# The last stage of a long convolution in two column tiles, with tokens on other partitions

## The chip, the cores and the metric

The kernel runs on one core of a Trainium2 chip. The metric is the device time of one execution in microseconds (us); the time before is the median of three runs. A profile of one execution goes with it.

## The reference

Two pairs of layers work on 2048 tokens of 512 channels in bf16. The first layer of a pair, A, is a gated long convolution; the second, B, is a layer norm, a matrix product to 1376, a gelu, and a product back to 512. Each layer norms its input first and adds its result to it. Both pairs have the same weights, and k and v do not depend on x, so the convolution's result y is the same in both pairs:

```python
def _A_ref(q, k, v, shift_k, ssm_k, ssm_D):
    ...
    kv = k_shift * v          # k after a causal filter of 4 taps per channel
    kv_f = rfft2(kv_pad); kf_f = rfft2(kf_pad)
    y = irfft2(kv_f * kf_f)[:, :S]      # causal convolution over all 2048 tokens
    y = y + kv * ssm_D
    return q * y

x = A_q
x = x + A(layernorm(x), A_k, A_v, ...)
x = x + B(layernorm(x), ...)
x = x + A(layernorm(x), A_k, A_v, ...)
x = x + B(layernorm(x), ...)
```

## The kernel before, in words

**Layout.** The tokens are taken in two halves of 1024 (h = 0 and 1). In a half, partition p holds the eight tokens 8p to 8p + 7 (`HALF`, L165): `xh[h]` is [128, 8, 512] and holds q, then x, up to the end. Because a partition's eight tokens are neighbours in DRAM, a load of q (`lx0`, `lx1`, L483) reads 128 runs of 8 KB that follow each other, and a store of the result (`st...`, L648) writes 128 rows of 1 KB, 8 KB apart. There are two such loads, and sixteen stores of 128 KB.

**The convolution.** The spectrum of a half is built in stages of small transforms, each a matrix product with a table (F, W, M, G; `_make_tables`). After the first stage (tables F) the data is regrouped: for the first half by transposes on TensorE (L345, L353), for the second by a write to a DRAM buffer (`first_stage_dram`, L357; `zd`, L375) and a regrouped read that brings it back in another order (L411 for the filter, L475 for kv). Then come the second stage (W, L428 and L497), the product with the filter's spectrum on VectorE (L511), the inverse second stage (M, L523), and a second regrouping, again by sixteen transposes on TensorE for the first half (L538) and by a write and a regrouped read in DRAM for the second (L530, L532).

**The last stage (L543 to L549).** For each half and each of four groups of 128 channels (cc) a block of sixteen matmuls with the table G fills one PSUM tile of [128, 8, 128] f32: for each of eight token places n, two matmuls (gh = 0 and 1) with 128 x 128 weights accumulate into the same 128 partitions. The weights of gh are zero in all columns but those of its own tokens: column 4a + 2gh + gl is the token group of output partition p. So a block is `Y{h}{cc}`, and there are eight. The tile is evacuated by one instruction on ScalarE or VectorE (L263, L265) into `ya(h, cc)`, where the gate of layer A (L591, L592) multiplies it by the normed x.

**The layers.** A half has two groups of 512 tokens. Norm statistics run on VectorE (L284), the power on GpSimd (L297), the norm is applied on ScalarE or VectorE (L304, L306), the normed tokens go through a DRAM buffer (L608) and a transposing transfer (L611), and then come the two matrix products (L623, L640), the gelu (L630) and the residual (L644).

**Order.** Nothing is scheduled at run time: `ORDER` (L16) lists all pieces by hand with their engine (P, D, A, G, S) and their PSUM or SBUF slots, and every engine works through its own pieces in that order. Nearly all transfers are on the queue of S (SyncE, SP in the profile). In that order `lx0.S` stands just ahead of `K1w0.S`, the last write of the filter's first stage, and `K1r0.S`, its regrouped read, follows the weights of layer B; `lx1.S` stands behind `U1w2.S` and ahead of `U1w1.S`, writes of kv's first stage. `lx1` goes where kv was, so it waits for all first-stage matmuls of that half. `KW101.P`, the first matmuls behind `K1r0`, stands in TensorE's order ahead of the last two of these.

Of the kernel before, what the change touches and what calls it, by code (L numbers as in the profile page):

```python
# [9 lines left out]
BF16 = mybir.dt.bfloat16  # L10
# [53 lines left out]
NK = 16  # L64
# [8 lines left out]
def _make_tables():  # L73
    a = np.arange(NA)
    k1 = np.arange(NA)
    psi = 2 * np.pi * np.outer(a, k1 + 0.25) / NA
    C, S = np.cos(psi), np.sin(psi)


    F = np.zeros((128, 2, 256))  # L80
    for g in range(4):
        r = 4 * a + g
        F[r, 0, g * 64:g * 64 + 32] = C
        F[r, 0, g * 64 + 32:g * 64 + 64] = S
        F[r, 1, g * 64:g * 64 + 32] = S
        F[r, 1, g * 64 + 32:g * 64 + 64] = -C


    W = np.zeros((128, NK, 128))

    M = np.zeros((128, NK, 2, 128))
    b = np.arange(NA)
    k2 = np.arange(NA)
    g, n = b // 8, b % 8
    for ka in range(NK):
        for par in range(2):
            phi = 2 * np.pi * ((16 * par + ka + 0.25) * b / 1024)[:, None] + 2 * np.pi * np.outer(b, k2) / NA
            c, s = np.cos(phi), np.sin(phi)
            rr = n * 16 + g * 4 + par
            ri = rr + 2  # L100
            m0 = par * 32
            W[rr, ka, m0:m0 + 32] = c
            W[rr, ka, 64 + m0:64 + m0 + 32] = s
            W[ri, ka, m0:m0 + 32] = -s
            W[ri, ka, 64 + m0:64 + m0 + 32] = c
            vr = (par * 4 + (g % 2) * 2) * 16 + (g // 2) * 8 + n
            vi = vr + 16
            for q, sign in ((0, 1.0), (64, -1.0)):
                rows = np.arange(q + m0, q + m0 + 32)
                M[np.ix_(rows, [ka], [0], vr)] = (sign * c.T / 32)[:, None, None, :]  # L110
                M[np.ix_(rows, [ka], [0], vi)] = (-sign * s.T / 32)[:, None, None, :]
                M[np.ix_(rows, [ka], [1], vr)] = (s.T / 32)[:, None, None, :]
                M[np.ix_(rows, [ka], [1], vi)] = (c.T / 32)[:, None, None, :]


    G = np.zeros((128, 2, 128))
    for gh in range(2):
        for gl in range(2):
            for par in range(2):
                r = np.arange(NK) * 8 + par * 4 + gl * 2  # L120
                k = 16 * par + np.arange(NK)
                cols = 4 * a + 2 * gh + gl
                G[np.ix_(r, [gh], cols)] = C[:, k].T[:, None, :] / 32
                G[np.ix_(r + 1, [gh], cols)] = S[:, k].T[:, None, :] / 32
    return tuple(_to_bf16_uint16(t) for t in (F, W, M, G))


# [26 lines left out]
def kernel(ctx: ExitStack, tc: tile.TileContext, A_q, A_k, A_v, A_shift_k, A_ssm_k, A_ssm_D,  # L154
                 B_x, B_w1, B_b1, B_w2, B_b2, out):
    nc = tc.nc
    P = 128
    _, S, D = A_q.shape
    F = B_w1.shape[1]
    KS = A_shift_k.shape[1]  # L160
    NT = 8
# [1 line left out]
    FT = (F + P - 1) // P  # L163
    FL = F - (FT - 1) * P
    HALF = "(h p n) d -> h p n d"  # L165
    q_d, k_d, v_d, out_d = (t.flatten_outer_dims().rearrange(HALF, h=2, p=P) for t in (A_q, A_k, A_v, out))
    K = 1024
    NPS, NZT, NXB, NTB = 4, 6, 3, 3

    def apf(t, offset, dims):  # L170
        tensor = t.tensor if isinstance(t, bass.AP) else t
        return bass.AP(tensor=tensor, offset=offset, ap=[[int(s), int(c)] for s, c in dims])

    F_np, W_np, M_np, G_np = _make_tables()
    F_h = nc.inline_tensor(F_np, name="tabF")
# [55 lines left out]
    sT = const.tile([P, CT, KS], BF16, name="sT")  # L231
    sF = const.tile([P, CT, KS], F32, name="sF")
    Ft = const.tile([P, 2, 2 * P], BF16, name="Ft")
    Gt = const.tile([P, 2, P], BF16, name="Gt")
    Wt = const.tile([P, NK, P], BF16, name="Wt")
    B1 = const.tile([P, FT], F32, name="B1")
    b1T = const.tile([P, FT], BF16, name="b1T")
# [29 lines left out]
    def queue(eng):  # L267
        return {"S": nc.sync, "A": nc.scalar, "G": nc.gpsimd}[eng]
# [50 lines left out]
    add = plan.add  # L319
    with tc.tile_pool(name="ps", bufs=1, space=bass.MemoryType.PSUM) as ps:  # L320
        pf = [ps.tile([P, 1024], F32, name=f"p{i}") for i in range(NPS)]

        def load(name, dst, src, nbytes, deps=(), **info):
            return add(name, "S", deps, lambda it: queue(it["eng"]).dma_start(dst, src), nbytes=nbytes, **info)
# [10 lines left out]
        def zt(it):  # L335
            return ZTb[it["slot"]["zt"]]
# [49 lines left out]
        lk = [load(f"lk{h}", kn[h], k_d[h], 2 ** 20) for h in range(2)]  # L386
        lv = [load(f"lv{h}", uv[h], v_d[h], 2 ** 20) for h in range(2)]
        lW = load("lW", Wt[:], W_h.ap().bitcast(BF16), 2 ** 19)
        lG = load("lG", Gt[:], G_h.ap().bitcast(BF16), 2 ** 16)

        KTe, KT = [[], []], [[], []]
        KSp, KUp = [[], []], [[], []]
# [87 lines left out]
                                         ring="zt"))  # L480
        names = {it["name"]: it for it in plan.items}
        USall = [[names[f"U{h}S{n}"] for n in range(NT)] if UD[h] else [names[f"U{h}{cc}S{q}"] for cc in range(CT) for q in range(2)] for h in range(2)]
        lx = [load(f"lx{h}", xh[h], q_d[h], 2 ** 20, (KSall[0] + KSall[1]) if h == 0 else USall[1]) for h in range(2)]  # L483


        YE = [[], []]
# [2 lines left out]
        for h in range(2):  # L489
            for cc in range(CT):  # L490
# [52 lines left out]
                def mms(o, te=te):  # L543
                    for n in range(NT):
                        for gh in range(2):
                            nc.tensor.matmul(o[:, n, :], Gt[:, gh, :], view(zt(te), [16, P])[:, gh * 8 + n, :], start=gh == 0, stop=gh == 1)
                _, ev = mm_evac(f"Y{h}{cc}", mms, [NT, P], lambda it, h=h, cc=cc: ya(h, cc), [te, lG], USall[0] if h == 0 else (),
                                free_mm=[(te, "zt")], units=16)
                YE[h].append(ev)  # L549
# [25 lines left out]
        for i, (l, g) in enumerate(seq):  # L575
# [59 lines left out]
            for t in range(4):  # L635
# [9 lines left out]
                res[(l, g, t)] = add(f"re{i}{t}", "D", [pe], resid, free=[(pe, "ps")], ns=690)  # L645
                mm2p[i].append(pe)
                if l == 1:
                    add(f"st{i}{t}", "S", [res[(l, g, t)]], lambda it, h=h, n=n0 + t: queue(it["eng"]).dma_start(out_d[h][:, n, :], xh[h][:, n, :]),  # L648
                        nbytes=2 ** 17)
        with tc.manual_schedule(engines={ENG.PE, ENG.Activation, ENG.DVE, ENG.Pool, ENG.SP}):  # L650
            plan.write(ORDER)
# [30 lines left out]
```

## Time and profile before

| | |
|---|---|
| median of three runs | 278.54 us (278.10 to 279.81) |
| the profiled execution's own time | 278.57 us |
| its span, first to last instruction | 276.8 us |
| TensorE matmuls busy | 254.5 us |
| VectorE busy | 185.0 us |
| ScalarE busy | 156.5 us |
| moved by DMA | 39.53 MB |
| matmuls of the last stage (L546) | 128, 8.5 us busy |

How to read the profile: PE is TensorE's matmuls, PEld its weight loads, DVE VectorE, ACT ScalarE, POOL GpSimd, SP SyncE; a q behind a name is the engine's sequencer, which waits or issues a transfer. The row of 40 digits cuts the span into 40 slices of 6.92 us; a digit is the busy share in tenths, for DMA the mean over 16 DMA engines. The chain of waits is followed back from the last instruction, at each step to what released it. A load's line in the kernel is that of the helper (L324). `arena` is the one large SBUF tile, `p` the PSUM tiles.

### The profile page before, as it was taken

The numbers are of one execution on the slowest core, as the hardware profiler recorded it, in microseconds if no ns is written. First come the engines' busy times: TensorE is split into PE (matmuls) and PEld (weight loads), VectorE is DVE, ScalarE is ACT, GpSimd is POOL, SyncE is SP. The second block draws the span as 40 slices with busy tenths as digits, with TensorE's granted clock in tenths as the row PEclk, the third lists the DMA queues.
The fourth block names the chain that finished last, engine by engine and source line by source line (L and its number), as shares of the span: only waits on it lengthen the run. The fifth ranks groups of instructions, "written<-read, shape, count | busy, mean of one in ns | idle before, by whom it ended". The sixth has DMA issues, their size and how long they took to land.

```text
span 276.8 us, 5232 instructions
## 1 busy us (share of the span) xinstructions
PE 254.5 (92%) x2112; PEld 159.7 (58%) x2112; DVE 185.0 (67%) x357; ACT 156.5 (57%) x197; POOL 50.7 (18%) x95
## 2 busy tenths in 40 slices
PE   2699999999765988999999898999999999999994
PEld 2599999679733644785766443444444444444441
DVE  0499688977995799999896879920039998001021
ACT  0366328998885997368982495276502741754300
POOL 3860000000502046321400124110002332000000
PEclk9999999999997999999999999999999999999999
DMA  6994093237999999987199803753000114601011
GB/s 165 400 417 188 2 227 78 93 138 244 346 217 278 324 211 193 176 195 132 40 233 230 109 2 115 211 147 60 2 0 0 40 66 116 159 3 38 11 49 54
DMA packets 48843, 39.53 MB, mean 143 GB/s; under 512 B 32850, under 2 KB 44212, under 8 KB 47412
## 3 DMA queue, kind: packets, MB, share of 16 engines
q1 hardware_dynamic: 48066, 39.07, 55.0%
q8 instruction: 16, 0.26, 0.4%
q10 hardware_dynamic: 674, 0.14, 0.3%
q0 software_dynamic: 80, 0.00, 0.1%
q14 instruction: 7, 0.06, 0.1%
HBM read 19.28 MB, written 12.06 MB: 113 GB/s over the span
## 4 chain that ended last, share of the span: by engine, by line
PE 68%; DMA 19%; DVE 6%; SPq 2%; ACT 2%; issue 1%; ACTq 0%
PE p L623 24%; PE p L640 22%; DMA arena<-zd 6%; PE p L463 5%; PE p L523 3%; DMA arena<-in_A_q_dram 3%; PE p L345 3%; DVE lst L284 3%; PE p L353 3%; PE p L365 2%; DMA zd<-arena 2%; DMA arena<-in_A_ssm_k_dram 2%; DMA arena<-vd 2%; DMA arena<-lnd 2%; PE p L428 2%; SPq L608 2%
## 5 line engine op out<-in xcount | busy, mean ns | idle before, releaser
L263 ACT ACTIVATE arena<-p 128x1024 bf16<-128x1024 f32 (+1 forms) x75 | 77.0, 1085 | 39.7 <-PE p L345 10.4
L640 PE MATMUL p<-arena 128*128 128x512 bf16 (+1 forms) x352 | 78.0, 379 | 2.3 <-ACT arena L630 2.3
L623 PE MATMUL p<-arena 128*128 128x512 bf16 (+1 forms) x352 | 77.8, 379 | 1.2 <-ACT arena L630 0.8
L630 ACT ACTIVATE arena<-p,B 128x512 bf16<-128x512 f32 (+1 forms) x88 | 54.6, 687 | 25.8 <-PE p L623 25.8
L297 POOL TENSOR_TENSOR lrs<-lrs,mhalf 128x2 f32<-128x2 f32 x32 | 28.6, 894 | 172.0 <-DVE lnm L294 172.0
L644 DVE TENSOR_TENSOR arena<-p,arena 128x512 bf16<-128x512 f32 x32 | 21.8, 688 | 56.8 <-PE p L640 56.7
L640 PEld LDWEIGHTS <-arena 128*128 128x128 bf16 (+1 forms) x352 | 34.1, 98 | 42.9 <-issue 2.9
L623 PEld LDWEIGHTS <-arena 128*128 128x128 bf16 (+1 forms) x352 | 35.0, 100 | 41.0 <-issue 1.0
L284 DVE BATCH_NORM_STATS2 lst<-arena 128x6 f32<-128x512 bf16 x64 | 41.0, 683 | 3.1 <-DMA arena<-in_A_q_dram 2.6
L304 ACT ACTIVATE arena<-arena,lnm,lrs 128x512 bf16<-128x512 bf16 x32 | 24.1, 813 | 30.2 <-POOL lnm L298 30.2
L511 DVE TENSOR_TENSOR arena<-arena 128x2048 bf16<-128x2048 bf16 x24 | 28.7, 1220 | 2.3 <-PE p L523 1.9
L265 DVE COPY arena<-p 128x2048 bf16<-128x2048 bf16 (+1 forms) x16 | 18.8, 1186 | 13.8 <-PE p L398 10.4
L523 PE MATMUL p<-arena 128*128 128x128 bf16 x384 | 24.1, 219 | 0.1
L265 DVE CAST arena<-p 128x1024 bf16<-128x1024 f32 x19 | 23.0, 1219 | 1.5 <-PE p L523 0.5
L523 PEld LDWEIGHTS <-arena 128*128 128x128 bf16 x384 | 22.4, 98 | 2.3 <-DVE arena L511 0.5
L463 PE MATMUL p<-arena 128*128 128x128 bf16 x256 | 15.4, 219 | 0.0
L463 PEld LDWEIGHTS <-arena 128*128 128x128 bf16 x256 | 14.8, 98 | 0.1
L428 PE MATMUL p<-arena,Wt 128*128 128x256 bf16 x64 | 9.5, 283 | 4.4 <-DMA arena<-zd 3.6
L306 DVE TENSOR_SCALAR arena<-arena,lrs,lnm 128x512 bf16<-128x512 bf16 x32 | 11.6, 408 | 2.8 <-POOL lnm L298 2.8
L365 PE MATMUL p<-arena,Ft 128*128 128x512 bf16 x48 | 12.7, 400 | 0.6 <-ACT arena L263 0.6
L591 DVE TENSOR_TENSOR arena<-arena 128x1024 bf16<-128x1024 bf16 x16 | 11.0, 688 | 2.8 <-ACT arena L263 1.7
L398 PE MATMUL p<-IDt,arena 128*128 128x128 bf16 x64 | 6.2, 269 | 7.0 <-DMA arena<-in_A_ssm_k_dram 7.0
(42 smaller groups left out, 168.8 us busy)
## 6 DMA issues: line engine op xcount, KB each, us to landing
arena<-arena SPq DMA_DIRECT2D x8, 512.0 KB, 8.5
zd<-arena SPq DMA_DIRECT2D x8, 512.0 KB, 5.0
lnd<-arena SPq DMA_DIRECT2D x14, 256.0 KB, 2.3
arena<-in_A_ssm_k_dram SPq DMA_DIRECT2D x8, 256.0 KB, 7.4
arena<-in_A_k_dram SPq DMA_DIRECT2D x2, 1024.0 KB, 8.3
arena<-in_A_v_dram SPq DMA_DIRECT2D x2, 1024.0 KB, 13.5
arena<-in_A_q_dram SPq DMA_DIRECT2D x2, 1024.0 KB, 6.6
arena<-zd SPq DMA_DIRECT2D x2, 1024.0 KB, 18.1
```

Source lines behind the costliest of these rows:

```text
L263: nc.scalar.activation(dst, src, AF.Copy)
L265: nc.vector.tensor_copy(dst, src)
L284: nc.vector.bn_stats(self.st[:, i, :], xg[:, i, :])
L297: nc.gpsimd.tensor_tensor(self.rs[:, a:b], self.rs[:, a:b], mhalf[:, a:b], ALU.pow)
L304: nc.scalar.activation(dst[:, i, :], xg[:, i, :], AF.Identity, bias=bi, scale=sc)
L463: nc.tensor.matmul(o[:, n, :], kT[:, cc, (n - t) % NT, c:c + P], DG[:, cc, t, :], start=t == 0, stop=t == KS - 1)
L511: nc.vector.tensor_tensor(Tb[it["slot"]["T"]], x2, kk, ALU.mult)
L523: nc.tensor.matmul(o[:, i, :], *ab, start=s == 0, stop=s == n - 1)
L623: nc.tensor.matmul(o[0:m, x, :], W1t[:, ct, ft * P:ft * P + m], lt[:, ct, :], start=ct == 0, stop=ct == CT - 1)
L630: nc.scalar.activation(ht[0:m, ft, :], o[0:m, x, :], AF.Gelu_apprx_tanh, bias=B1[0:m, ft:ft + 1])
L640: nc.tensor.matmul(o, ht[0:m, ft, t * P:t * P + P], W2t[0:m, ft, :], start=ft == 0, stop=ft == FT - 1)
L644: nc.vector.tensor_tensor(xg[:, t, :], view(pf[pe["slot"]["ps"]], [D]), xg[:, t, :], ALU.add)
```

## The change

The two halves of the output columns (gh) become two column tiles of TensorE's array. One table G of 64 columns serves both: column 32gl + a. The matmul of gh writes PSUM partitions 64gh to 64gh + 63, each matmul starts and ends its own accumulation, and none adds to another's result. There are still sixteen matmuls in a block, each with its weight load, of 64 columns in place of 128.

So token group 4a + 2gh + gl now lies on partition 64gh + 32gl + a. For the gate, q has to lie in the same way, and the result goes back from there. `token_rows` describes it on the DRAM side: four groups, 8 tokens apart, of 32 rows, 32 tokens apart. k and v stay as they were, as do all earlier stages. Layer B and the norms work token by token, whatever the order of tokens on the partitions is.

The order of all instructions on all engines is unchanged; other than the matmuls of L546 and their weight loads, the load of G, the two loads of q and the sixteen stores, the instructions are the same.

```diff
-    G = np.zeros((128, 2, 128))
-    for gh in range(2):
-        for gl in range(2):
-            for par in range(2):
-                r = np.arange(NK) * 8 + par * 4 + gl * 2
-                k = 16 * par + np.arange(NK)
-                cols = 4 * a + 2 * gh + gl
-                G[np.ix_(r, [gh], cols)] = C[:, k].T[:, None, :] / 32
-                G[np.ix_(r + 1, [gh], cols)] = S[:, k].T[:, None, :] / 32
+    G = np.zeros((128, 64))
+    for gl in range(2):
+        for par in range(2):
+            r = np.arange(NK) * 8 + par * 4 + gl * 2
+            k = 16 * par + np.arange(NK)
+            cols = 32 * gl + a
+            G[np.ix_(r, cols)] = C[:, k].T / 32
+            G[np.ix_(r + 1, cols)] = S[:, k].T / 32
...
-    q_d, k_d, v_d, out_d = (t.flatten_outer_dims().rearrange(HALF, h=2, p=P) for t in (A_q, A_k, A_v, out))
+    k_d, v_d = (t.flatten_outer_dims().rearrange(HALF, h=2, p=P) for t in (A_k, A_v))
...
+    def token_rows(t, h, n0, n9):
+        return apf(t, (h * 1024 + n0) * D, [[8 * D, 4], [32 * D, 32], [1, (n9 - n0) * D]])
...
-    Gt = const.tile([P, 2, P], BF16, name="Gt")
+    Gt = const.tile([P, P // 2], BF16, name="Gt")
...
-        lG = load("lG", Gt[:], G_h.ap().bitcast(BF16), 2 ** 16)
+        lG = load("lG", Gt[:], G_h.ap().bitcast(BF16), 2 ** 15)
...
-        lx = [load(f"lx{h}", xh[h], q_d[h], 2 ** 20, (KSall[0] + KSall[1]) if h == 0 else USall[1]) for h in range(2)]
+        lx = [load(f"lx{h}", xh[h], token_rows(A_q, h, 0, NT), 2 ** 20, (KSall[0] + KSall[1]) if h == 0 else USall[1]) for h in range(2)]
...
-                            nc.tensor.matmul(o[:, n, :], Gt[:, gh, :], view(zt(te), [16, P])[:, gh * 8 + n, :], start=gh == 0, stop=gh == 1)
+                            nc.tensor.matmul(o[64 * gh:64 * gh + 64, n, :], Gt[:, :], view(zt(te), [16, P])[:, gh * 8 + n, :], start=True, stop=True)
...
-                    add(f"st{i}{t}", "S", [res[(l, g, t)]], lambda it, h=h, n=n0 + t: queue(it["eng"]).dma_start(out_d[h][:, n, :], xh[h][:, n, :]),
+                    add(f"st{i}{t}", "S", [res[(l, g, t)]], lambda it, h=h, n=n0 + t: queue(it["eng"]).dma_start(token_rows(out, h, n, n + 1), xh[h][:, n, :]),
```

## The prediction

> **What bounds the kernel now.** I read the page first (busy shares, the 40 slices, the shares of the chain), then the chain of waits in order of time, then the windows by stage.
>
> ```profile
> span 276.8 us, 5232 instructions
> PE 254.5 (92%) x2112; PEld 159.7 (58%) x2112; DVE 185.0 (67%) x357; ACT 156.5 (57%) x197; POOL 50.7 (18%) x95
> ...
> DMA  6994093237999999987199803753000114601011
> ...
> PE 68%; DMA 19%; DVE 6%; SPq 2%; ACT 2%; issue 1%; ACTq 0%
> ```
>
> TensorE is busy for 92% of the span and gives 68% of the chain; DMA gives 19%. The DMA row is nearly solid nines from its eleventh slice to its seventeenth (69 to 118 us): in the middle the bound is the transfers, not TensorE. The chain of waits, in order of time (start, us, what), says which ones:
>
> ```profile
> 62.20 6.71 DMA zd<-arena
> 68.98 16.11 DMA arena<-zd
> 85.13 1.03 PE p L428 x4
> ...
> 87.90 8.49 DMA arena<-in_A_q_dram
> ...
> 96.41 1.29 DVE lst L284 x2
> ...
> 126.57 6.24 PE p L623 x28
> ...
> 134.60 0.89 PE p L546 x16
> ...
> 149.06 0.52 PE p L546 x10
> 149.58 6.12 DMA arena<-vd
> ...
> 155.74 1.07 PE p L546 x16
> ...
> 158.54 0.89 PE p L546 x16
> ...
> 273.02 0.69 DVE arena L644
> ```
>
> A write of the first stage to DRAM (L375), its regrouped read (L411), four matmuls that waited for it, then the second load of q (8.49 us), then VectorE's statistics on that load: all of this one behind the other, up to 126.57, when TensorE becomes the chain. From there it is matmuls but for one wait for a regrouped read (149.58). The four L546 rows are the last stage's blocks of the second half (h=1), the only ones of its eight on the chain; a residual at 273.02 and a store end it.
>
> The load of q is not only waited for. All these transfers are issued by SP:
>
> ```profile
> 61.08 0.33 SPq L324 DMA_DIRECT2D arena<-in_A_q_dram  x1
> 62.20 0.32 SPq L375 DMA_DIRECT2D zd<-arena  x1
> ...
> 66.60 1.74 SPq L324 DMA_DIRECT2D arena<-in_B_w_dram  x2
> 68.98 10.87 SPq L411 DMA_DIRECT2D arena<-zd  x2
> ...
> 87.90 0.33 SPq L324 DMA_DIRECT2D arena<-in_A_q_dram  x1
> 88.33 2.84 SPq L375 DMA_DIRECT2D zd<-arena  x2
> ...
> 99.11 7.06 SPq L475 DMA_DIRECT2D arena<-zd  x3
> ...
> 124.49 0.58 SPq L532 DMA_DIRECT2D arena<-vd  x1
> ```
>
> The first load of q (61.08) goes out just ahead of the chain's write (62.20); the weights (66.60) follow and then the regrouped read (68.98), which waits for that write. The second (87.90) goes out just ahead of two writes (88.33) that the reads at 99.11 wait for. So q's bytes stand in front of chain bytes twice.
>
> ```profile
> core 0: us, PE busy (x) PEld busy (x) DVE busy (x) ACT busy (x) POOL busy (x), PEclk, DMA share, GB/s
> 13.50:20.50 7.00, 7.00 (x110) 6.84 (x109) 6.63 (x8) 4.84 (x4) 4.91 (x10) 1.00 1.02 416
> 62.20:69.00 6.80, 6.80 (x124) 6.80 (x122) 5.19 (x7) 6.05 (x6) 0.00 (x0) 1.00 0.77 243
> 87.90:96.40 8.50, 7.44 (x57) 5.02 (x57) 5.18 (x7) 8.50 (x11) 0.00 (x0) 0.97 1.02 343
> 96.40:112.50 16.10, 14.00 (x91) 7.30 (x89) 15.84 (x43) 13.99 (x21) 7.52 (x12) 1.00 1.17 195
> ...
> 273.70:276.80 3.10, 0.00 (x0) 0.00 (x0) 0.01 (x1) 0.00 (x0) 0.00 (x0) 0.89 0.12 42
> ```
>
> The last two columns are the mean busy share of 16 DMA engines, and GB/s. Where the inputs stream (13.50) one engine moves 416 / (1.02 x 16) = 25.5 GB/s; in the window of the second load 343 / (1.02 x 16) = 21.0. In the window of the first load the engines are idle for a share of 0.23, that is 1.6 of 6.80 us; from 87.90 to 112.50 they have no idle time. VectorE is busy for 15.84 of 16.10 us behind the second load: a delay at 96.41 is passed on.
>
> **The change, part by part.** First the transfers. token_rows turns the DRAM side of the two loads (L483) and the sixteen stores (L648) from 128 rows one after another into 4 groups of 32 rows with a stride; the on-chip side stays 128 partitions, and each row keeps its length (8 KB for a load, 1 KB for a store). In the changed kernel's instruction list the stores read 4x32x512 where they read 128x512. Bytes and number of pieces are the same; what can change is how a transfer is divided among the 16 engines. No transfer of before has a leading dimension of 4, so I bound it. One end: divided as before, 64 KB of a load on each engine, 65,536 / 25.5 = 2.6 us: no cost. Other end: the leading dimension is what is divided, so at most four engines get a share, 256 KB each: 262,144 / 25.5 = 10.3 us, or 12.5 at 21.0 GB/s. I take four shares. The nearest rows are the window's 1.02 of share at 416 GB/s, of transfers that all lead with 128 on both sides, and the regrouped reads of L411 and L475, whose DRAM side is written with a dimension of 16 in front: every wide transfer of this code leads with a multiple of 16 on both sides, and these are the first that don't.
>
> [...]
>
> Each load then keeps its engines for 10.3 - 2.6 = 7.7 us longer (12.5 - 3.1 = 9.4 at the lower rate).
>
> ```profile
> DMA to landing us min/median/max: 6.6/6.6/6.6
> ...
> DMA to landing us min/median/max: 1.9/1.9/3.2
> ```
>
> The first row is the first load of q (6.6 us), the second the stores (1.9 at best). A store has 8 KB on each engine, 0.3 us of its 1.9, so some 1.6 us are fixed.
>
> - First load. The write at 62.20 and the read at 68.98 have their parts on the same four engines behind it. At most the delay is 9.4; at least it is the bare load, 1.6 + 10.3 = 11.9, less 6.6 = 5.3. I take 7.7 less the 1.6 us of idle time in that window: 6.1 us on the chain, at 85.13.
> - Second load. At most 9.4; at least 11.9 - 8.49 = 3.4, if nothing stands before it. VectorE waits for it, and TensorE waits for the writes behind it (88.33, then 99.11). I take 4.6, nearer to the low end, since 8.49 is far above the bare 1.6 + 2.6 and part of it is a queue that a delay of the stage drains.
> - VectorE's statistics on the first load start as late as that load; what is queued behind them there (evacuations of the transposes of the first half, then L546) has until 85.13, when TensorE waited 3.55 us for the regrouped read.
>
> ```profile
> 75.67 2.18 PE L546 MATMUL p<-arena,Gt 128*128 128x128 bf16 x32 [1.49 <-DVE arena L265]
> ...
> 85.13 1.03 PE L428 MATMUL p<-arena,Wt 128*128 128x256 bf16 x4 [3.55 <-DMA arena<-zd]
> ```
>
> It costs nothing while that read is late by as much, and up to 7.7 less that 3.55, 4.2 us, if it is not.
> - Stores. Only the last one ends the span. It has 32 KB on each of four engines in place of 8: 24,576 bytes at 42 / (0.12 x 16) = 21.9 GB/s, 1.1 us. The others lie beside matmuls, where the DMA row shows sixes and less; without that cover each costs the same 1.1.
> - Issue. A transfer in a new form may take SP longer to issue: 0.33 us each now; the nearest with a split side is 0.58 (L532, one issue). 0.25 at the last store, taken as nothing.
>
> The table G shrinks from 64 to 16 KB; it is wanted at 68 us and was loaded in the first ten. Nothing.
>
> Second, the last stage, L546. Sixteen matmuls a block stay sixteen, with weights of 64 columns, to PSUM partitions 0 to 63 and 64 to 127 in turn, each complete by itself instead of accumulated in pairs.
>
> ```profile
> L353 PEld LDWEIGHTS <-arena 128*128 128x128 bf16 x128 | 9.0, 148 | 0.2
> ...
> L546 PEld LDWEIGHTS <-Gt 128*128 128x128 bf16 x128 | 7.6, 98 | 4.0 <-issue 2.0 <-DMA arena<-vd 1.5
> ...
> L623 PEld LDWEIGHTS <-arena 128*96 128x96 bf16 x32 | 3.9, 123 | 3.6 <-DMA arena<-lnd 0.6
> ```
>
> ```profile
> L546 PE MATMUL p<-arena,Gt 128*128 128x128 bf16 x128 | 8.5, 219 | 2.6 <-DVE arena L265 1.5 <-DMA arena<-vd 1.0
> ```
>
> ```profile
> 15.69 1.00 PE p L353 x16
> ```
>
> Before, a block takes 0.89 us (55.6 ns a matmul), with the weight loads hidden. If the two tiles work side by side, a pair takes the time of one and a block 0.45: over the four blocks of the chain (0.89 + 0.52 + 1.07 + 0.89 = 3.37) a gain of 1.7. The four of the first half are covered by the wait at 85.13 (3.55 us). If they do not, the loads may show: a load of 96 columns lasts 123 ns against 98 for 128, and matmuls behind loads of 148 ns (L353) come every 62.5 ns (16 in 1.00 us), +0.11 a block; one matmul of 219 ns that overlaps nothing at each end of a block adds 2 x 0.16. That is +0.43 a block, 1.7 in all. I take -0.8, half the gain: the streams can halve, but there are as many instructions and loads as before.
>
> [...]
>
> Nothing else moves: the order of the instructions is the same on every engine.
>
> Sum, against the profiled execution's 278.57 us (its span 276.8 and 1.8 around it; the median of the three runs is 278.54, so no shift): 278.57 + 6.1 + 4.6 + 1.1 - 0.8 = 289.6 us.
>
> **Rivals.**
> - The loads stay divided among 16 engines; only the last stage changes. For it: the pieces and the on-chip side are the same. Against it: no wide transfer here leads with fewer than 16. Then 278.57 - 0.8 = 277.8 us (276.9 to 278.6): not slower. It decides where a load keeps its engines for no more than the 1.6 us longer that the first window has free: 41 KB more on an engine, ten shares in place of sixteen.
> - The same, and the column tiles cost: 278.57 + 1.7 = 280.3 us.
> - Four engines, but the first delay is covered: the chain's write and read overtake the load. Against it: the write took 6.71 us, longer than it needs for half a megabyte at 416 GB/s (1.3) and the fixed 1.6, so it does wait behind the load. Then 278.57 + 3.4 + 1.1 - 0.8 = 282.3.
>
> **How the numbers follow.** Four engines with both delays: 0.70, predicted 289.6, its own range 284 to 299 (low ends 5.3 + 3.4 with the gain of 1.7 give 286.7, and some cover that I do not see; high ends 9.4 + 9.4 + 1.1 + 1.7 give 300.2). Divided as before: 0.16 with a gain, 0.06 with costs. First delay covered: 0.08. About 1% (2.8 us) is what a measurement of this kernel can tell from no change. Slower by more: 0.69 of the first and 0.06 of the last, 0.75; within: 0.01 + 0.13 + 0.06 + 0.02 = 0.22; faster: 0.03, a gain that the rows do not give. The range has to take in both signs: 277.5 to 298, which leaves out a few hundredths at each end.
>
> **What would show it.** The load of q in the chain or in the view by tile: 10 us and more from issue to landing, against 6.6 and 8.49, is four engines; 6 to 9 is not. The regrouped read's matmul moves from 85.13 to about 91, VectorE's statistics from 96.41 to about 107, and the DMA share of those windows falls below 1 although the chain waits for DMA. The last store's end lies 1.1 us further behind the last residual. A block of L546 in TensorE's timeline: 0.45 us is two tiles side by side, 0.9 and more is not. I am wrong if the loads land as before, or if they are late and TensorE's chain from 126.57 on is not.

## The result, and the profile after

| | before | changed |
|---|---|---|
| median of four runs each, one chip | 278.32 us (276.66 to 279.81) | 311.16 us (310.70 to 312.52) |
| the profiled execution | 278.57 us, span 276.8 | 310.92 us, span 309.2 |
| mean granted clock of TensorE | 0.993 | 0.946 |

The ratio is 1.122 (95% interval 1.117 to 1.128): 32.8 us slower. A ratio, here and below, is of the runs within 1.5% of the fastest of their kernel; a median takes all runs. The prediction, 289.6 us with a range to 298, had the sign and the place, and a third of the size. The profile after, first the page (the kernel has two more lines above here, so L546 of before is L548, L284 is L286, and so on):

```profile
span 309.2 us, 5209 instructions
PE 255.9 (83%) x2089; PEld 158.2 (51%) x2112; DVE 184.8 (60%) x357; ACT 156.0 (50%) x197; POOL 49.7 (16%) x95
...
PE   2799999995027894089999979898999999989993
...
PEclk9999999999558999679999988999999999999998
DMA  7991571358599682797906990366300014531011
...
PE 54%; DMA 25%; DVE 14%; ACT 3%; issue 1%; SPq 1%; ACTq 0%
```

TensorE works as long as before (255.9 us); the span has grown around it. DMA's share of the chain went from 19 to 25%, VectorE's from 6 to 14%. The solid nines that the DMA row had from its eleventh slice on are broken up by a five, a six, an eight, a two and sevens: the chain waits for DMA more while its engines do less. The clock row has fives in its eleventh and twelfth slice (77 to 93 us), where the row of TensorE falls to 0 and 2. Now the chain of waits (start, us, what):

```profile
61.15 21.57 DMA arena<-in_A_q_dram
82.74 1.29 DVE lst L286 x2
...
89.45 2.35 DVE arena L267 x2
...
100.25 22.81 DMA arena<-in_A_q_dram
123.08 1.29 DVE lst L286 x2
...
182.64 0.64 PE p L548 x16
...
205.61 4.46 DMA lnd<-arena
210.12 4.90 DMA arena<-lnd
...
259.49 5.28 DMA arena<-lnd
...
304.01 0.69 DVE arena L646
```

Both loads of q now stand in the chain with 21.57 and 22.81 us, and behind each of them VectorE's statistics. Follow the delay by setting rows against those of before. The second stage's first matmul (L430) starts at 97.79 rather than 85.13 in TensorE's timeline: 12.7 us late after the first load. The statistics on the second load start at 123.08 rather than 96.41: 26.7 late, of which 12.4 is its later issue (100.25 against 87.90) and 14.3 its longer duration (22.81 against 8.49). A last-stage block of the second half is as late, 182.64 against 155.74 (26.9). The last residual is at 304.01 rather than 273.02 (31.0), and behind it the span goes on for 4.5 us rather than 3.1. So 26.7 come with the loads, some 4.3 between 183 us and the end, and 1.4 behind the last residual.

How the first load passes its delay on stands in the waits (us in all, times, longest) and in the timeline of SP:

```profile
DVE lst L286 <- DMA arena<-in_A_q_dram: 31.9, 2, 16.5
...
PE p L548 <- DVE arena L267: 17.0, 1, 17.0
...
SPq L413 <- DMA zd<-arena: 2.8, 1, 2.8
```

```profile
61.15 0.73 SPq L326 DMA_DIRECT2D arena<-in_A_q_dram  x1
...
66.67 14.17 SPq L326 DMA_DIRECT2D arena<-in_B_w_dram  x2
83.81 9.17 SPq L413 DMA_DIRECT2D arena<-zd  x2
```

VectorE stood still for 16.5 us in front of the statistics on one load (2.6 us on both, before), and TensorE then 17.0 us for an evacuation that stands behind them in VectorE's order. And SP itself was held: its two issues of weights (66.67), 1.74 us before, now take 14.17. The regrouped read of the filter, issued at 68.98 before, goes out at 83.81. The hold is not what made it late: SP was free again at 80.84 and then waited 2.8 us more (the last of the three waits) for the write to `zd`, which was issued behind the load, at 62.28, and landed some 21.4 us later (6.71 in the chain before). What comes late is that write.

```profile
69.00:82.70 13.70, 4.58 (x80) 4.41 (x80) 0.00 (x0) 4.08 (x4) 0.00 (x0) 0.83 0.70 136
82.70:100.25 17.55, 7.76 (x51) 3.94 (x52) 16.80 (x46) 9.83 (x11) 4.57 (x11) 0.65 0.96 240
115.00:123.00 8.00, 4.12 (x18) 1.82 (x18) 0.00 (x0) 2.84 (x5) 0.00 (x0) 1.00 0.24 80
```

In the last window only the second load is under way: the engines' mean share is 0.24, as much as four of sixteen, at 80 / (0.24 x 16) = 20.8 GB/s each. From 69.00 to 82.70, with the weights beside the load, 136 / (0.70 x 16) = 12.1 GB/s for each busy engine, by the same division. The prediction had taken 25.5. The last column but two is the clock: 0.65 behind VectorE's first wait (0.97 and 1.00 in the windows of before behind 87.90), and 0.50 in the 2.3 us behind TensorE's (90.70 to 93.00).

And the last stage itself, in the groups by shape (after the bar: us busy, ns of one):

```profile
L548 PE MATMUL p<-arena,Gt 128*64 128x128 bf16 x128 | 6.4, 255 | 19.4 <-DVE arena L267 17.0 <-DMA arena<-vd 2.2 <-ACT arena L265 0.2
```

The 128 matmuls are busy for 6.4 us in place of 8.5, though one lasts 255 ns in place of 219: two blocks of the first half fall behind the wait, where the clock is 0.50 and they take 2.20 us together (from 90.72); a block of the second half, at a clock of 1.00, takes 0.64 (182.64).

### The profile page after: what moved, and what is told of

Same layout as the page of the kernel before. It is cut to its first block, busy times and chain, and to the rows that moved or that the text cites. A ratio compares the mean times of both kernels' runs of the same rounds, so it can differ in the third digit from the quotient of the medians.

```text
span 309.2 us, 5209 instructions
## 1 busy us (share of the span) xinstructions
PE 255.9 (83%) x2089; PEld 158.2 (51%) x2112; DVE 184.8 (60%) x357; ACT 156.0 (50%) x197; POOL 49.7 (16%) x95
## 4 chain that ended last, share of the span: by engine, by line
PE 54%; DMA 25%; DVE 14%; ACT 3%; issue 1%; SPq 1%; ACTq 0%
PE p L625 17%; PE p L642 15%; DMA arena<-in_A_q_dram 14%; DVE lst L286 6%; PE p L525 4%; PE p L465 4%; DMA arena<-lnd 3%; PE p L367 3%; PE p L355 3%; PE p L347 3%; DMA vd<-arena 2%; DMA arena<-in_A_ssm_k_dram 2%; DMA arena<-vd 2%; PE p L499 2%; ACT arena L265 2%; DMA lnd<-arena 1%
## 5 line engine op out<-in xcount | busy, mean ns | idle before, releaser
L625 PE MATMUL p<-arena 128*128 128x512 bf16 (+1 forms) x343 | 78.7, 383 | 3.8 <-DMA arena<-lnd 1.7
L642 PE MATMUL p<-arena 128*128 128x512 bf16 (+1 forms) x342 | 79.3, 385 | 2.8 <-ACT arena L632 2.3
L286 DVE BATCH_NORM_STATS2 lst<-arena 128x6 f32<-128x512 bf16 x64 | 41.0, 683 | 32.3 <-DMA arena<-in_A_q_dram 31.9
L299 POOL TENSOR_TENSOR lrs<-lrs,mhalf 128x2 f32<-128x2 f32 x32 | 27.6, 862 | 201.6 <-DVE lnm L296 201.6
L267 DVE COPY arena<-p 128x2048 bf16<-128x2048 bf16 (+1 forms) x16 | 18.8, 1186 | 11.3 <-PE p L400 10.7
L548 PE MATMUL p<-arena,Gt 128*64 128x128 bf16 x128 | 6.4, 255 | 19.4 <-DVE arena L267 17.0
L499 PE MATMUL p<-arena,Wt 128*128 128x128 bf16 x128 | 9.4, 230 | 10.4 <-DMA arena<-zd 10.4
L548 PEld LDWEIGHTS <-Gt 128*64 128x64 bf16 x128 | 5.0, 131 | 21.8 <-issue 17.5
L499 PEld LDWEIGHTS <-Wt 128*128 128x128 bf16 x128 | 8.5, 103 | 11.5 <-issue 10.7
L367 PE MATMUL p<-arena,Ft 128*128 128x512 bf16 x44 | 12.6, 399 | 1.5 <-ACT arena L265 1.0
```

Of the source, the lines that this page charges most:

```text
L267: nc.vector.tensor_copy(dst, src)
L286: nc.vector.bn_stats(self.st[:, i, :], xg[:, i, :])
L299: nc.gpsimd.tensor_tensor(self.rs[:, a:b], self.rs[:, a:b], mhalf[:, a:b], ALU.pow)
L499: nc.tensor.matmul(o[:, i, :], Wt[:, k0 + i, :], view(zt(zx), [NK, P])[:, k0 + i, :], start=True, stop=True)
L625: nc.tensor.matmul(o[0:m, x, :], W1t[:, ct, ft * P:ft * P + m], lt[:, ct, :], start=ct == 0, stop=ct == CT - 1)
L642: nc.tensor.matmul(o, ht[0:m, ft, t * P:t * P + P], W2t[0:m, ft, :], start=ft == 0, stop=ft == FT - 1)
```

## Experiments

All ratios are to the kernel before on the same chip.

**1. Whose delay is it? The four parts one by one.** Theory: the DRAM side that leads with 4 puts each transfer on four engines, and the two loads, one behind the other on the chain, are the loss. Rival: the last stage or the new order of the result costs something of its own. In four kernels a transfer is cut into four, each of 32 partitions, with a DRAM side led by 32 rows; what is computed is the same.

```diff
-        lx = [load(f"lx{h}", xh[h], token_rows(A_q, h, 0, NT), ...) for h in range(2)]
+        for j in range(4):       # all_spread, loads_spread; first_ and second_spread: one of the two loads
+            queue(it["eng"]).dma_start(xh[h][32 * j:32 * j + 32], apf(A_q, (h * 1024 + 8 * j) * D, [[32 * D, 32], [1, NT * D]]))
...
-     queue(it["eng"]).dma_start(token_rows(out, h, n, n + 1), xh[h][:, n, :])
+     for j in range(4):          # all_spread
+         queue(it["eng"]).dma_start(apf(out, (h * 1024 + n + 8 * j) * D, [[32 * D, 32], [1, D]]), xh[h][32 * j:32 * j + 32, n, :])
```

> The changed kernel, but each load of q and each store is cut into four transfers of 32 partitions whose DRAM side leads with 32 rows; rows, strides, table and column tiles as in the change. Theory (a transfer led by 4 runs on four DMA engines, and that is the whole loss): both loads land in 6 to 9 us again, and the time is that of before less the blocks' gain, 276.5 to 278 us. Rival (the stride of 32 tokens between rows is what is slow, or the column tiles): the loads stay above 15 us and the time above 300.

Measured: 283.56 us, ratio 1.020 (1.014 to 1.026).

> Only the two loads are cut into four transfers of 32 partitions; the sixteen stores stay as changed, led by 4. Theory: 1 to 2 us over the kernel with all of them cut, since only the last store lies on the end (277.5 to 279.5 us). Rival (the stores on four engines hold up the transfers of the second pair of layers behind them on the queue): 282 us and more.

Measured: 284.75 us, ratio 1.026 (1.020 to 1.032).

> Only the first load of q is cut into four transfers of 32 partitions; the second load and the stores stay led by 4. Theory (the two delays of 15.0 and 14.3 us follow each other on one chain): 311.2 less 15 to 16, 295 to 296 us. Rival (one delay covers a part of the other): below 290 here, or hardly less than 311 here with the first delay hidden.

Measured: 295.04 us (two runs), ratio 1.062 (1.050 to 1.074).

> Only the second load of q is cut into four transfers of 32 partitions; the first load and the stores stay led by 4. Theory (two delays in a row): 311.2 less 14 to 15, 296 to 297 us. Rival (the delays overlap): the savings of this and of the kernel with only the first load cut do not add up to that of both.

Measured: 295.39 us (two runs), ratio 1.063 (1.055 to 1.071).

The theory holds for the loads: cut in four they land 4.5 to 7.6 us after their issue in all_spread, and with both spread, 311.16 - 284.75 = 26.4 us go. One late load alone costs 10.3 or 10.6 us (295.04 and 295.39 less 284.75), so the two cost some 5.5 more together than apart (the times of a pair of runs lie up to 4 us apart); why was not tried. But the rest was expected to be nearly nothing, and 5 to 6 us stay: all_spread misses its 276.5 to 278, and loads_spread falls to its rival, stores that hold up what stands behind them. The chain of loads_spread and SP's timeline in all_spread show where:

```profile
177.39 5.40 DMA lnd<-arena
182.81 4.73 DMA arena<-lnd
```

```profile
174.75 3.92 SPq L654 DMA_DIRECT2D out_dram<-arena  x8
...
179.26 3.66 SPq L654 DMA_DIRECT2D out_dram<-arena  x8
182.97 2.00 SPq L617 DMA_TRANSPOSE arena<-lnd  x1
```

The same stretch of the kernel before:

```profile
178.43 0.93 SPq L648 DMA_DIRECT2D out_dram<-arena  x2
180.07 2.05 SPq L611 DMA_TRANSPOSE arena<-lnd  x1
```

In the form of the change, stores on four engines (the last of the changed kernel, alone from 306.00 to 307.50, has a DMA share of 0.25 to 0.27) stand ahead of a write of normed tokens (5.40 us until it landed, 2.3 in the median before) and of the transposing transfer behind it. Cut in four, they hold SP: the eight issues of a pair of stores take 3.92 and 3.66 us, where the two of before took 2.13 and 0.93, and the transposing transfer (L611 before, 180.07) goes out at 182.97. Either way layer B's next group begins late.

**2. Are the stores the rest?** plain_stores is loads_spread with the stores in their form of before.

```diff
-     queue(it["eng"]).dma_start(token_rows(out, h, n, n + 1), xh[h][:, n, :])
+     queue(it["eng"]).dma_start(apf(out, (h * 1024 + n) * D, [[8 * D, P], [1, D]]), xh[h][:, n, :])
```

> Both loads cut into four transfers of 32 partitions, and the sixteen stores written in the form of before (128 rows of 1 KB, 128 in front), so that the rows of the result land at other tokens' places; bytes and pieces are the same. Theory (the stores on four engines, and the many issues of cut stores, hold SP's queue in front of the transposing transfers): 276.5 to 277.5 us, 7 under the kernel with cut loads and changed stores. Rival (the column tiles or the cut loads cost it): 282 us and more.

Measured: 279.11 us, ratio 1.001 (0.998 to 1.005), and no transfer of layer B's tokens is left in its chain behind 126 us. The stores' term is 284.75 - 279.11 = 5.6 us by the medians, close to the 4.3 and 1.4 found above. These lie on two chips, though, and by the ratios (1.026 and 1.001) it is nearer 7 us. The theory's 276.5 to 277.5 was not reached: by this run the tiles and the cut loads together gain nothing.

**3. How does the first load's delay travel?** The prediction had it go through the queue, by the regrouped read; the chain after shows it through VectorE. In stats_late, on second_spread, VectorE's statistics on the first load and what depends on them stand behind the evacuations that TensorE waits for:

```diff
- ... sa10.D ... sa12.D pa10.G ... sa02.D ... kvm10.D
+ ... kvm10.D sa10.D sa12.D sa02.D pa10.G sa00.D pa12.G pa02.G pa00.G aa02.D
```

> The kernel with only the second load cut, with the statistics on the first load and what follows from them moved behind the evacuations and the product that VectorE owes the last stage of the first half (and one apply moved from ScalarE to VectorE). Theory (the first delay reaches the chain through VectorE, which waits for that load in order; the regrouped read behind the load on SP's queue is some 4 to 5 us less late): 295.4 less 4 to 5, 290 to 292 us. Rival A (only VectorE passes the delay on): 282 to 285. Rival B (only the queue does, as the prediction had it): 294 to 296.

Measured: 293.92 us in the profiled run, 300.17 in a second one.

```profile
63.06 20.33 DMA zd<-arena
83.46 13.35 DMA arena<-zd
96.86 1.04 PE p L428 x4
```

The expectation fell. VectorE's way is gone from the chain, and the queue's way takes its place almost as late: the write behind the load takes 20.33 us (6.71 before), and the second stage starts at 96.86, against 98.72 in second_spread. So mending VectorE's way gives 1.9 us at this place, and at most 1.5 in the time (293.92 against 295.39, on another chip): the queue's way alone keeps nearly the whole delay, 11.7 us at this place where the changed kernel has 12.7.

**4. Is it the leading dimension?** Back to the kernel before, without column tiles, with only the DRAM side of the loads written in another form:

```diff
-        lx = [load(f"lx{h}", xh[h], q_d[h], ...
+        lx = [load(f"lx{h}", xh[h], apf(A_q, h * 1024 * D, [[8 * D, 16], [128 * D, 8], [1, NT * D]]), ...     # lead16
+        lx = [load(f"lx{h}", xh[h], apf(A_q, h * 1024 * D, [[8 * D, 8], [64 * D, 16], [1, NT * D]]), ...      # lead8
+        lx = [load(f"lx{h}", xh[h], apf(A_q, h * 256 * D, [[512 * D, 4], [8 * D, 32], [1, NT * D]]), ...      # runs4
```

> The kernel before with both loads of q in one transfer each whose DRAM side is 16 groups of 8 strided rows, so the rows of q lie on other partitions than the rest of the work expects; bytes and pieces as before. Theory (the leading dimension sets the number of engines): 16 engines, loads as before, 277 to 279.5 us. Rival (rows in a stride, or a form with a split side, are slow): loads of 12 us and more, above 285.

Measured: 280.46 us, one run, against 279.29 for the kernel before. Its loads land after 8.0 and 9.72 us (6.6 and 8.49 before).

> The kernel before with both loads of q in one transfer each whose DRAM side is 8 groups of 16 strided rows (q's rows on other partitions than the rest expects). Theory (eight engines, 128 KB on each, at the 14 GB/s an engine that the change's loads show): 9.4 us of packets and 3 us around them, loads of 11 to 13 us, 284 to 290 us. Rival (four groups are a case of their own; the rest uses all engines): as with sixteen groups, loads of 8 to 10 us and 278 to 281 us.

Measured: 290.76 us, one run, against 278.14.

> The kernel before with both loads of q led by 4 groups of 32 rows that follow each other in DRAM, so that each engine reads 256 KB in one run (other rows of q than the rest expects). Theory (few engines is all there is; rows in a stride cost nothing more): first load 19 to 22 us, 301 to 306 us (the change's 311 less what its stores cost). Rival (the stride of 32 KB between an engine's rows halves its rate): first load 12 to 14 us, 288 to 293.

Measured: 302.83 us, one run, against 278.14. The loads of lead8, then of runs4:

```profile
61.23 14.76 DMA arena<-in_A_q_dram
...
94.52 12.96 DMA arena<-in_A_q_dram
```

```profile
59.98 21.73 DMA arena<-in_A_q_dram
...
99.76 19.70 DMA arena<-in_A_q_dram
```

Among these forms the leading number sets the loss: sixteen is nearly harmless (1 us, within the noise), eight costs 12.6 us, four 24.7, in a kernel that has no column tiles at all. runs4 lies within its theory; lead16 and lead8 are 1 us above theirs, and lead8's first load, 14.76, is above 11 to 13. In runs4 each group's 256 KB are one run of DRAM, and the first load takes as long as in the changed kernel (21.73 and 21.57), the second 3.1 us less (19.70 and 22.81). So the stride isn't what makes them slow.

**5. Why 21 us and not 10?** Open was whether the four engines were slow because they shared with the weights, or because of the form. Two kernels add three loads of q to the kernel before, in its idle time at 187 us, each waiting for the one ahead; a third moves the weights in the changed kernel.

```diff
+        probe_t = place([P, NT, D], 0)
+        load("pr2", probe_t, apf(A_q, 0, [[8 * D, 4], [32 * D, 32], [1, NT * D]]), 2 ** 20)     # quiet_4; quiet_8: 16, then 8
...
- ... w4.S w2.S V001.P3 w1.S V000e.A2 K1r0.S ... K1r1.S Y02.P2 w3.S
+ ... V001.P3 V000e.A2 K1r0.S ... K1r1.S w4.S w2.S w1.S w3.S Y02.P2     # weights_later
```

> The kernel before with three further loads of a half of q (1 MB each) into an area of SBUF that nothing reads any more, at about 187 us, where its DMA engines are idle: twice led by 128 rows, then led by 4, each waiting for the one before. They cost some time of their own; only their durations are wanted. If the four engines were slow in the changed kernel because they also moved the weights and the regrouped data, the one led by 4 takes about 14 us alone (256 KB at 20.8 GB/s and 1.6 fixed), and the one led by 128 takes 4 to 5. If the form itself is slow, whatever else runs, it takes 20 us and more here too.

> As the kernel with three further loads of q in the idle time, but led by 128, then 16, then 8. If a piece costs the same in every form, the one led by 16 takes as long as the one led by 128 (4 to 5 us) and the one led by 8 takes about 8. If the split form doubles the time of a piece, 16 takes about 8 and 8 takes about 14.

> The changed kernel with the three transfers of layer B's weights moved on SP behind the two regrouped reads of the filter. If the first load of q took 21.6 us because its four engines also moved weights and SP stood blocked behind it, it now lands in 13 to 16 us, SP issues the regrouped read within a few us of the write's landing, and the second stage's first matmul starts at about 91 rather than 97.8. If the form itself is slow, the load still takes 20 us and more. The weights are then late or stand in front of the second load, so the total may be anything from 300 to 315 us.

The windows of quiet_4 (the whole of one led by 128 and its best microsecond, then the one led by 4), then of quiet_8 (16, then 8):

```profile
195.00:199.00 4.00, 4.00 (x20) 1.85 (x19) 0.00 (x0) 2.96 (x5) 0.00 (x0) 1.00 0.73 258
...
197.00:198.00 1.00, 1.00 (x6) 0.47 (x5) 0.00 (x0) 0.54 (x2) 0.00 (x0) 1.00 1.01 418
202.00:214.00 12.00, 12.00 (x57) 5.40 (x56) 8.09 (x21) 0.99 (x2) 1.77 (x4) 1.00 0.24 66
...
217.00:218.00 1.00, 1.00 (x7) 0.45 (x5) 1.00 (x2) 0.54 (x2) 0.86 (x2) 1.00 0.06 16
218.00:219.00 1.00, 1.00 (x6) 0.43 (x5) 0.96 (x7) 1.00 (x2) 0.35 (x1) 1.00 0.00 0
```

```profile
193.00:197.00 4.00, 4.00 (x20) 1.77 (x19) 0.35 (x1) 2.02 (x4) 0.00 (x0) 1.00 1.05 244
200.00:210.00 10.00, 10.00 (x48) 4.49 (x46) 6.83 (x19) 0.40 (x1) 1.76 (x4) 1.00 0.49 105
210.00:211.00 1.00, 1.00 (x6) 0.49 (x5) 0.97 (x2) 1.00 (x2) 0.00 (x0) 1.00 0.00 0
```

Rate of each busy engine, GB/s over 16 times the share: led by 128, 418 / (1.01 x 16) = 25.9 at best and 258 / (0.73 x 16) = 22.1 over the whole load; by 16, 244 / (1.05 x 16) = 14.5; by 8, 105 / (0.49 x 16) = 13.4; by 4, 66 / (0.24 x 16) = 17.2. The load led by 4 was issued at 199.99 and moved bytes until 217 to 218: some 17.5 us with nothing beside it. Led by 128 it had taken 5.5 us (issued at 194.53, the next one, which waits for it, at 199.99), by 16 it took 7.1 (191.63 to 198.73), and by 8 some 11.3 (198.73 to 210): quiet_8 lies between its two expectations. So the form is slow by itself: over whole loads, three fifths to four fifths of an engine's 22.1. That is most of what was missing, and above the 14 us that quiet_4's expectation gave to four engines alone. The total cost is small (279.02 and 275.61 us, one run each), since nothing waits there.

In weights_later (311.07 us, one run) the first load, without the weights, takes 17.97 us, as in quiet_4, and 3.6 less than in the changed kernel. The regrouped read goes out at 80.06 and the second stage starts at 93.95 (97.79 in the changed kernel). SP was free from 62.34 on and waited 17.6 us for the write to `zd`: the load on four engines holds that write up, whatever SP issues. The total gains nothing, because the weights then stand in front of the second load:

```profile
60.90 17.97 DMA arena<-in_A_q_dram
...
96.41 25.90 DMA arena<-in_A_q_dram
```

So a first load of 21.57 us is 17.5 to 18 of its form and 3.6 of company. The expectation of 13 to 16 fell.

A split DRAM side may not be what it takes for the slow rate. In the window of the first load, 62.20 to 69.00, the kernel before moves 243 GB/s at a share of 0.77, 19.7 for each busy engine; all_spread, whose transfers have no split side but 32 partitions each, needs 0.97 for 233, 15.0:

```profile
62.20:69.00 6.80, 6.80 (x127) 6.61 (x125) 3.86 (x4) 6.06 (x6) 0.00 (x0) 1.00 0.97 233
```

Other transfers run in that window, so this is a sign and no measurement of the form.

Why one engine moves fewer bytes in these forms was not shown.

**6. Can the tiles be had without the loss, and do they gain?** With column 2a + gl of G for token group 4a + 2gh + gl, a half of the partitions holds 32 pairs of neighbouring groups, and each transfer is two of 64 partitions, led by 32.

```diff
-            cols = 32 * gl + a
+            cols = 2 * a + gl
...
-    def token_rows(t, h, n0, n9):
-        return apf(t, (h * 1024 + n0) * D, [[8 * D, 4], [32 * D, 32], [1, (n9 - n0) * D]])
+    def token_rows(t, h, gh, n0, n9):
+        return apf(t, (h * 1024 + 16 * gh + n0) * D, [[32 * D, 32], [8 * D, 2], [1, (n9 - n0) * D]])
```

> The columns of G in another order (2a + gl), so that a load or a store is two transfers of 64 partitions whose DRAM side leads with 32; column tiles as in the change. Theory: loads as before; a store takes two issues of 0.4 us in place of one, so less is lost at SP's queue than with four: 278 to 281 us. Rival (a transfer of 64 partitions uses fewer engines than one of 128): loads above 9 us and the time above 283.

Measured: 280.14 us, ratio 1.003 (0.999 to 1.007), as the theory had it. Its twice as many stores stand ahead of the transposing transfers as in all_spread, so in two more kernels eight of them were moved on SP behind `dr5` and `dr7`, with the tiles and, as a control, in the kernel before:

```diff
- ... dr4.S ab32.A ... st22.S ... st20.S ... st23.S ... st21.S ... dr5.S
+ ... dr4.S ab32.A ... dr5.S st22.S st20.S st23.S st21.S                  # and st5x behind dr7
```

> The kernel with the columns of G in the other order and two transfers for each load and store, and with the eight stores of the second and fifth group moved on SP's queue behind the transposing transfers that they stood in front of. Theory (the blocks' gain of 1 us at 177 us is lost again at SP's queue): 276 to 278 us, 0.5 to 1% under before. Rival (the stores do not matter there, or the gain is lost elsewhere): 278.5 and more.

Measured: 278.74 us (12 runs), ratio 1.003 (0.999 to 1.006).

> The kernel before with the same eight stores moved, as a control: no column tiles. Theory (its stores take one issue of 0.33 us each and hold nothing up for long): within 0.5% of before. Rival (moving the stores is the gain, not the tiles): as much under before as the kernel with column tiles.

Measured: 276.82 us (12 runs), ratio 0.995 (0.993 to 0.998).

So the complete versions with tiles only come back to the kernel before: two_pieces_late misses its 276 to 278, and is 1.9 us above its control on the same chip. What takes the tiles' gain there was not found. Last, the tiles alone: the kernel before with nothing but G and L546 changed, loads and stores in their old form.

```diff
-    nc.tensor.matmul(o[:, n, :], Gt[:, gh, :], view(zt(te), [16, P])[:, gh * 8 + n, :], start=gh == 0, stop=gh == 1)
+    nc.tensor.matmul(o[64 * gh:64 * gh + 64, n, :], Gt[:, :], view(zt(te), [16, P])[:, gh * 8 + n, :], start=True, stop=True)
```

> The kernel before with the two column tiles in L546 and the small table G, and nothing else: loads and stores have their form of before, so the gate meets q of other tokens and rows go to other tokens' places. It isolates the blocks' term of the sum. If the blocks' gain reaches the end, as the prediction had it, the ratio is 0.994 to 0.998 (0.8 to 1.7 us). If what a block gains is taken up by the next wait behind it, or given back by the weight loads, it is 1.000 within the interval.

Measured: ratio 0.993 (0.989 to 0.997); median of 12 runs 278.41 us, 274.86 to 280.75, against 278.65.

> tiles_only with the eight stores of before_late moved behind dr5 and dr7. If the stores ahead of the transposing transfers are what swallows the blocks' gain, it beats before_late by 0.8 to 1.7 us (ratio to before about 0.990). If nothing reaches the end, it equals before_late (0.995).

Measured: ratio 0.993 (0.990 to 0.997); median 277.63 us.

> before_late again, on the same chip as tiles_only_late, so that the two can be compared: 0.995 of before.

Measured: ratio 1.000 (0.997 to 1.003); median 278.41 us.

By the ratios the tiles alone gain between 0.8 and 3 us, in both kernels. But the mean over all 12 runs of tiles_only is 1.0 us below that of before, with an error of 1.3, and the medians are 0.2 apart. So the sign agrees with the prediction's term, but neither it nor the size is clear of the noise. Moving the stores gained 0.5% on one chip and nothing on the other, where 0.995 was expected again, and nothing on top of the tiles: not settled. No complete version with column tiles beat the kernel before.

## Why the prediction was wrong, step by step

- **Transfers on four engines.** Right. A share of 0.24 with the second load alone is that of four engines of sixteen, and the leading number sets it: 0.49 of share, eight, for 8 and 1.05, all sixteen, for 16 (quiet_8), with times to match (lead8, runs4). The four shares that the sum is worked out with were the author's choice: no row of before showed them.
- **What four engines cost: the step that failed.** "262,144 / 25.5 = 10.3 us" took the rate at which one engine moves whole transfers led by 128. Led by 4 it is 17.2 GB/s over a whole load alone (20.8 in the last 8 us of the changed kernel's second load, 12.1 beside the weights), which makes 262,144 / 17.2 = 15.2 us of it; the bare load is 17.5 us, not 11.9, and 21.6 and 22.8 in company, where the high ends were 6.6 + 9.4 = 16.0 and 8.49 + 9.4 = 17.9. Both bounds of the two largest terms came from rows of another form. The upper one should have been left open, as nothing in the trace showed a split transfer's rate.
- **First load, 6.1 at the second stage's first matmul.** Measured 12.7. The regrouped read did become late through the queue, as forecast (by 11.7 even where VectorE is out of the way), because the write ahead of it waited behind the load: it took some 21.4 us, and 7.91 in all_spread, where the load is cut in four. That SP would be held for 14.17 us at its next issues wasn't forecast; at the read it cost little, as that had to wait for the write until 83.81 in any case.
- **VectorE's statistics, "nothing while that read is late by as much, and up to 4.2".** Wrong in its bound, since it was built on 7.7 us of delay: they waited for 16.5, and TensorE for them 17.0. Because the read is nearly as late, their own part in the sum is only 1 to 2 us (stats_late).
- **Second load, 4.6.** Measured 14.0 on top of the first (26.7 - 12.7). The two together, 10.7 forecast, are 26.4 by loads_spread.
- **Stores, only the last, 1.1.** The last was right in size: the tail grew by 1.4. "The others lie beside matmuls" was wrong: some stand on SP's queue ahead of writes and transposing transfers that TensorE then waits for (205.61 to 215.02, and 259.49), 4.3 us in all. Together 5.6 to 7 by plain_stores.
- **Blocks, -0.8.** Close in size. The two tiles do run side by side: a block lasts 0.64 us, of which 0.22 is the last matmul, so one starts on average every (0.64 - 0.22) / 15 = 28 ns, against (1.06 - 0.22) / 15 = 56 before. But each end of a block loses something. The same block of the first half in tiles_only, then before, each between matmuls of the stage ahead of it:

```profile
67.19 1.95 PE L525 MATMUL p<-arena 128*128 128x128 bf16 x32
69.08 0.64 PE L548 MATMUL p<-arena,Gt 128*64 128x128 bf16 x16
69.64 1.07 PE L525 MATMUL p<-arena 128*128 128x128 bf16 x16
```

```profile
66.37 1.95 PE L523 MATMUL p<-arena 128*128 128x128 bf16 x32
68.15 1.06 PE L546 MATMUL p<-arena,Gt 128*128 128x128 bf16 x16
69.05 1.06 PE L523 MATMUL p<-arena 128*128 128x128 bf16 x16
```

From the first matmul ahead to the block it is 1.89 us against 1.78, 0.11 more; from the block to the next matmul 0.56 against 0.90, where sixteen of 28 ns would be 0.45. So a block gains 0.23 us rather than 0.45, some 0.9 for the four of the chain. The prediction had taken half the gain as a middle between two bounds; that the half is right is in part luck. In tiles_only the 128 matmuls are busy for 5.1 us, 8.5 before:

```profile
L548 PE MATMUL p<-arena,Gt 128*64 128x128 bf16 x128 | 5.1, 221 | 3.5 <-DVE arena L267 2.6 <-DMA arena<-vd 0.7 <-ACT arena L265 0.2
...
L548 PEld LDWEIGHTS <-Gt 128*64 128x64 bf16 x128 | 4.0, 109 | 5.4 <-issue 3.4 <-DMA arena<-vd 1.7
```

The weight loads of 64 columns take 109 ns against 98 for 128 and stay hidden within a block, whose matmuls start every 28 ns. That they take longer needn't come from the column tiles: the loads of 96 columns took 123 ns before, without any. What takes the 0.11 us at each end of a block was not shown.
- **Not forecast: the clock.** The granted clock is 0.67 behind the second load, as this row of the same windows shows, and 0.50 in the 2.3 us behind TensorE's wait of 17.0 us (90.70 to 93.00). There the work ran slower: 1.10 us for a block of L548, 0.64 at a clock of 1.00. What the clock costs in the whole time wasn't measured.

```profile
123.00:138.60 15.60, 6.50 (x37) 3.78 (x37) 15.27 (x43) 4.41 (x6) 7.52 (x12) 0.67 0.94 178
```

The terms as measured: loads 26.4, stores 5.6 to 7, blocks about -1 (not separable in the kernels with cut loads): 31 to 32 of the 32.8 us.

## What to carry to other kernels

The leading dimension of the DRAM side decided here how many DMA engines moved a transfer (shares of 0.24, 0.49 and 1.05 for 4, 8 and 16), and in each of these forms an engine was slower too (17.2, 13.4 and 14.5 GB/s against 22.1): before a layout is changed for the matmul's sake, its transfers are to be counted by engines, and a form that the trace doesn't show is to be timed alone in an idle stretch of the same kernel, which costs one run. A slow transfer on SP was paid for by what stood behind it on that queue (14.17 us at two issues of weights; 20.33 us for a write in stats_late, 6.71 before) and by the engines that waited for it in order (VectorE 16.5 us, TensorE behind it 17.0). So a gain of 0.2 us a block needs the layout's transfers to stay as they were.

## What the hardware showed that was not expected

- One engine's rate fell from 22.1 GB/s over a whole load (25.9 at best) to 14.5 and 13.4 when the same 1 MB was led by 16 or 8 on the DRAM side, and was 17.2 led by 4, with no other transfer beside it.
- SP was held at an issue: two issues of weights took 14.17 us behind a load on four engines (1.74 before).
- Sixteen issues of small stores take SP some 0.47 us each (3.92 and 3.66 us for eight), and a transposing transfer behind them goes out 2.9 us later than before.
- Two column tiles start a matmul every 28 ns on average rather than 56, but a block of sixteen loses 0.11 us at each end, half of what it could gain.
